# One kernel of attention and expert routing: the embedding loaded from another queue, fewer warming transposes, and a new hand-written order of steps

## The chip, the cores and the metric

The kernel runs on one core of a Trainium2 chip. A core has five engines with a queue of instructions each: TensorE (PE in the rows below; its weight loads are PEld), VectorE (DVE), ScalarE (ACT), GpSimd (POOL) and SyncE (SP), which here only issues transfers. The metric is the time of one execution in device microseconds; less is better. A difference is read against the runs of the kernel before, which lie between 472.85 and 473.6 us.

## The reference

Causal attention over 4 batches, 12 heads, 448 positions and 64 columns; its output, seen as 1792 tokens of 768 columns, goes through a layer of 8 experts, of which each token uses one.

```python
scores = scale * np.matmul(q, k.transpose(0, 1, 3, 2))
scores = np.where(mask, -1000000000.0, scores)
attn = np.exp(scores - np.max(scores, axis=-1, keepdims=True))
attn = attn / (np.sum(attn, axis=-1, keepdims=True) + 1e-09)
x = np.matmul(attn, v)                 # then laid out as 1792 x 768
...
xn = x / (np.linalg.norm(x, axis=-1, keepdims=True) + 1e-06)
en = expert_emb / (np.linalg.norm(expert_emb, axis=-1, keepdims=True) + 1e-06)
logits = xn @ en.T / tau
expert_idx = np.argmax(logits, axis=1)
...
for e in range(E):                     # w1: 768 x 1024, w2: 1024 x 768 for each expert
    mask = expert_idx == e
    h = np.maximum(x[mask] @ w1[e], 0.0)
    out[mask] = gate_w[mask, None] * (h @ w2[e])
```

## The kernel before

The work has two halves. In the first, 24 pairs of heads (numbered 0 to 23, six to a batch) go through attention, four chunks of 112 query rows each. In the second, the tokens, sorted by expert, go in tiles of 128 through the two weight matrices.

No scheduler sets the order. The string ORDER is a list of tokens such as `V3x.12/A` or `S1.4:0`: a step's name, a pair, after a slash the engine (A ScalarE, V VectorE, G GpSimd) where a step can be done by several, after a colon the PSUM banks. A loop at the end of `attn_moe` (L1001) calls the steps one after the other, and each engine runs its own instructions strictly in that order, waiting where a tile is not ready.

The steps of a pair `p`, chunk `i` and head `h`: `LDr`, `LDv` load queries with keys, and values (`LDa` is the first half of pair 0's `LDr`). `hi` and `lo` on GpSimd split the late columns into a rounded part and a rest (pairs 1 to 20). `S0` to `S3`, `S02` are the score products on TensorE. `M{i}{h}` on VectorE adds the mask and takes the row maximum out of PSUM. `E{i}{h}` on ScalarE is the exponential with its sum. `T0`, `T2`, `T3` transpose the result on TensorE into two tiles each, and `V0x`, `V0y` and so on copy these out of PSUM, on ScalarE or VectorE. `PV0` to `PV3` are the products with the values, `VO` copies their result, `RC` takes reciprocals of the sums, `X` turns the output to tokens and adds the products with the embedding, and `XE`, `LE` on VectorE scale both. Before that the embedding's norm is taken once: `EE` loads the embedding and tau on SP's queue, `es0` squares and sums on ScalarE, `es1` takes a first guess and two Newton steps of a square root on VectorE, `es2` to `esA` finish it.

At the end of a batch `R0` to `Rc` find each token's expert and its rank (`RK`, `CN` on TensorE). After the third batch `Z` picks the expert with the most tokens; its first matrix is loaded and split in six parts `k` (`LW` load, `W` rounded part on ScalarE, `Wl` rest: GpSimd for k below 5, VectorE for k = 5), and `Y`, `YP`, `YI`, `YG` gather a first tile of its tokens. `XTa` to `XLb` turn and split that tile. `F0` to `F5` are its first product on TensorE: `F0` to `F3` use part k of the weights, `F4` parts 4 and 5 for the first half of the columns, `F5` the same for the second. `RL` copies the halves out, `HT` transposes them, `HH` and `HL` split them. `A`, `B` split the second matrix (loads `LL`) on ScalarE and VectorE, `G1` to `G6` are parts of the second product. In between, on VectorE, `N0` to `Nc` work out the sorted place of every token, `TB` on TensorE turns that into a list, `IG` makes it integer, `GA` gathers the second tile, `xta` to `xlb` turn and split it. `Q` are sums of squares on ScalarE. From there on `body(t)` runs per tile, its order set by the code.

At the very start 16 transposes of the identity keep TensorE busy before the first scores (L999).

Of the kernel before, what the change touches and what calls it, by code (L numbers as in the profile page):

```python
# [45 lines left out]
V3y.1/V es4.0 M10.3 hi.3 V3x.1/A lo.3 S3.3:2 M11.3 es5.0 E31.2 S02.3:0 es6.0 M30.3 E01.2 hi.4 E20.2 T3.2:1 es7.0 M01.3
M20.3 es8.0 M31.3 lo.4 E11.2 PV0.1:6 PV1.1 V3x.2/A PV2.1 M21.3 PV3.1 RC.0/G E21.2 LDv.2 E00.2 es9.0:2 M00.3 E10.2
esA.0 T2.2:2 RC.1/G V3y.2/A VO.0/A T0.2:0 V2y.2/A V0y.2/A V2x.2/V S02.4:1 V0x.2/V LDr.7 X.0:2 M00.4 E01.3 M21.4 S3.4:0
PV0.2:7 E11.3 M01.4 E10.3 E20.3 E31.3 LE0.0 PV1.2 LDv.3 E30.3 LE1.0 XE1.0 M20.4 E00.3 E21.3 XE0.0 PV2.2 M30.4 M31.4
VO.1/V T3.3:1 RC.2/G lo.5 LDv.4 S1.4:0 V3y.3/V M11.4 M10.4 T0.3:2 PV3.2 V0y.3/V V3x.3/A S1.5:1 E20.4 V0x.3/A LDr.8  # L50
T2.3:0 S3.5:2 VO.2/A E21.4 V2y.3/A M10.5 E10.4 M11.5 E11.4 V2x.3/V M30.5 S02.5:1 M31.5 hi.6 lo.6 PV0.3:6 M21.5 M00.5
M01.5 X.1:2 E30.4 E00.4 M20.5 XE1.1 E11.5 E30.5 E01.4 T2.4:0 X.2:1 V2y.4/V LDv.5 E00.5 RC.3/G PV1.3 V2x.4/V XE1.2
LE1.2 E31.4 LE0.1 LDr.9 PV2.3 E01.5 LE0.2 XE0.1 E10.5 PV3.3 LE1.1 T0.4:0 XE0.2 V0x.4/A V0y.4/V T3.4:2 V3y.4/V V3x.4/A
S1.6:1 hi.8 M10.6 M11.6 S3.6:0 M31.6 S02.6:2 hi.7 E20.5 E21.5 M30.6 T0.5:1 PV0.4:7 M01.6 E31.5 M20.6 V0x.5/A M21.6
lo.7 T2.5:0 M00.6 V0y.5/A V2y.5/V T3.5:1 S02.7:2 RC.5/G VO.3/A V2x.5/A RC.4/G LDr.10 lo.8 V3x.5/A V3y.5/A S3.7:0 E01.6
M00.7 E30.6 M01.7 M21.7 E20.6 M20.7 M30.7 X.3:1 M31.7 LE1.3 XE1.3 S1.7:2 M11.7 XE0.3 PV1.4 PV2.4 PV3.4 E10.6 E11.6
LDv.6 E00.6 E21.6 M10.7 LE0.3 PV0.5:6 hi.9 T0.6:1 E31.6 V0y.6/A V0x.6/A LDr.11 VO.4/V T2.6:0 V2x.6/A X.4:2 V2y.6/V
E00.7 T3.6:1 E11.7 S02.8:0 PV1.5 E10.7 V3x.6/A E01.7 LDv.7 V3y.6/A PV2.5 lo.9 XE0.4 LE1.4 M00.8 M01.8 RC.6/G PV3.5
M20.8 XE1.4 LE0.4 E31.7 LDv.8 E00.8 S1.8:2 S3.8:1 M21.8 VO.5/V M11.8 X.5:0 M10.8 T0.7:2 XE1.5 PV0.6:7 E21.7 E21.8
LE0.5 hi.11 M31.8 E10.8 E20.7 PV1.6 E30.7 V0y.7/A LE1.5 V0x.7/V PV2.6 XE0.5 hi.10 E20.8 M30.8 PV3.6 T3.7:0 LDr.12  # L60
T2.7:2 VO.6/V V3x.7/A V3y.7/V V2y.7/A V2x.7/V S3.9:1 S02.9:0 M31.9 M30.9 E30.8 M01.9 E01.8 lo.10 S1.9:2 E31.8 q0.5
M11.9 E11.8 E01.9 PV0.7:7 hi.12 T3.8:1 M10.9 M21.9 X.6:2 R0.5:6 PV1.7 PV2.7 V3x.8/A V3y.8/A E30.9 PV3.7 XE0.6 RC.7/G
T0.8:1 M00.9 q3.5 q2.5 LE1.6 XE1.6 WX.5 q1.5 E31.9 LE0.6 M20.9 VO.7/A V0x.8/V LDr.13 T2.8:2 V0y.8/A V2x.8/A E11.9
E20.9 S3.10:0 V2y.8/V S02.10:1 E21.9 M30.10 M00.10 M01.10 LDv.10 E00.10 RC.8/G S1.10:2 PV0.8:7 M11.10 M31.10 M21.10
PV1.8 PV2.8 LDv.9 PV3.8 E00.9 lo.12 R1.5 E10.9 M20.10 T0.9:0 M10.10 R2.5 lo.11 R3.5 E21.10 S1.11:1 R4.5 X.7:2 M11.11
# [1116 lines left out]
```

## Time and profile before

| | us |
|---|---|
| time, median of 3 runs | 473.51 (472.85 to 473.6) |
| the profiled execution's own time | 474.17 |
| its span, first to last instruction | 472.0 |
| TensorE busy | 454.4 (96%) |
| VectorE busy | 349.3 (74%) |
| ScalarE busy | 295.9 (63%) |
| GpSimd busy | 158.0 (33%) |

The shares are means over stages that differ. Until about 160 us ScalarE, VectorE and TensorE are all close to full; after that TensorE alone is. A busy TensorE is not TensorE at its peak, since the modelled end of a matmul covers the time its result takes to come out.

### The profile page before, as it was taken

To read this page: it belongs to the slowest core of one execution; us is meant where nothing else is said; L and a number is where in the kernel's file an instruction comes from. 1 tells how busy PE (TensorE), PEld (TensorE's weight loads), DVE (VectorE), ACT (ScalarE), POOL (GpSimd) and SP (SyncE) were. 2 spreads that over 40 slices of the span, in tenths; PEclk is the share of its full clock that TensorE was granted. 3 is DMA by queue.
4 is the path that set the end of the run, shared out by engine and by line. 5 is a ranking of instruction groups with operands and counts; after the bars stand their busy time and mean duration, and the time that the engine had idled before them with its cause. 6 is when DMAs were issued, how large, how long until landed. Compare 5 with 4: busy or idle time off the path is not lost. (4 is left out here: it accounts for less than half of the span.)

```text
span 472.0 us, 12320 instructions
## 1 busy us (share of the span) xinstructions
PE 454.4 (96%) x3948; PEld 380.9 (81%) x3948; DVE 349.3 (74%) x1024; ACT 295.9 (63%) x731; POOL 158.0 (33%) x158
## 2 busy tenths in 40 slices
...
GB/s 181 206 102 92 169 179 120 138 216 118 150 134 276 269 124 97 69 33 164 174 378 294 296 52 267 76 392 223 301 330 227 110 69 56 284 180 283 286 250 38
DMA packets 27779, 87.35 MB, mean 185 GB/s; under 512 B 2710, under 2 KB 3670, under 8 KB 27680
## 3 DMA queue, kind: packets, MB, share of 16 engines
...
## 5 line engine op out<-in xcount | busy, mean ns | idle before, releaser
L425 ACT ACTIVATE aq<-aq,mx 112x224 f32<-112x224 f32 (+3 forms) x192 | 99.9, 529 | 2.4 <-DVE mx L420 2.3
...
L420 DVE CUSTOM_DVE_ANT_0 aq<-bank,ar 112x224 f32<-112x224 f32 (+3 forms) x192 | 76.0, 441 | 12.1 <-PE bank L415 10.6
L458 PE MATMUL bank<-ap 112*64 112x448 f32 (+3 forms) x384 | 53.2, 409 | 0.0
L721 DVE STREAM_TRANSPOSE turned<-fa 32x256 f32<-32x256 f32 x112 | 48.8, 436 | 1.8 <-DVE akr L733 0.3
L822 ACT COPY fa<-bank 128x512 f32<-128x512 f32 x28 | 15.2, 588 | 54.4 <-PE bank L763 40.3
L626 POOL DMA_INDIRECT fa<-xd,ig x21 | 23.7, 1129 | 62.8 <-PE bank L694 51.2
L443 PEld LDWEIGHTS bank<-idt,aq 64*112 64x112 f32 (+1 forms) x960 | 33.2, 131 | 13.9 <-ACT aq L425 4.4
L1030 DVE TENSOR_TENSOR wl<-fa,wh 128x1024 fp32r<-128x1024 f32 x36 | 41.5, 1218 | 3.1 <-PE bank L764 1.6
L447 ACT COPY ap<-bank 112x384 f32<-112x384 f32 (+2 forms) x91 | 39.5, 474 | 3.2 <-PE bank L443 1.6
L443 PE MATMUL bank<-idt,aq 48*112 48x48 f32 (+1 forms) x960 | 38.6, 219 | 2.3 <-ACT aq L425 1.0
L458 PEld LDWEIGHTS bank<-ap 112*64 112x64 f32 x384 | 23.8, 136 | 20.7 <-issue 12.6
L425 ACT ACTIVATION_READ_ACCUMULATOR aq<-aq,mx 112x1 f32 x192 | 37.8, 197 | 0.0
L1029 ACT CAST wh<-fa 128x1024 fp32r<-128x1024 f32 x36 | 34.9, 1048 | 3.5 <-PE bank L765 1.6
L763 PE MATMUL bank<-wh,akr 128*128 128x512 f32 x84 | 33.0, 393 | 0.0
L765 PE MATMUL bank<-wh,apr 128*128 128x512 f32 x84 | 32.9, 391 | 0.0
L765 PE MATMUL bank<-wh,akr 128*128 128x512 f32 x84 | 32.8, 391 | 0.0
L397 POOL TENSOR_TENSOR wl<-ak,wh 128x672 fp32r<-128x672 f32 x20 | 32.4, 1626 | 1.1
L764 PE MATMUL bank<-wl,akr 128*128 128x512 f32 x84 | 32.8, 391 | 0.0
L764 PE MATMUL bank<-wl,aor 128*128 128x512 f32 x84 | 32.8, 390 | 0.0
L763 PE MATMUL bank<-wh,aor 128*128 128x512 f32 x84 | 32.7, 389 | 0.0
L415 PE MATMUL bank<-ak 64*112 64x224 f32 (+3 forms) x224 | 31.3, 359 | 0.5 <-DVE ar L492 0.3
(320 smaller groups left out, 1172.8 us busy)
## 6 DMA issues: line engine op xcount, KB each, us to landing
...
```

Of the source, the lines that this page charges most:

```text
L397: step("lo", SPLIT)(lambda p: g.tensor_tensor(los[p % 3], late(p), his[p % 3], op=ALU.subtract))
L420: v.tensor_tensor_reduce(out=Ps[p % 2][i, h], in0=st.pop(("sp", p, i, h)), in1=mask[i], scale=-0.125, scalar=3e38, op0=ALU.add, op1=ALU.mi ...
L425: ac.activation(x, x, AF.Exp, bias=mxs[p % 3][:, h, i : i + 1], scale=-1.0, accum_out=sums[p % 3][:, h, i : i + 1])
L443: pe.transpose(t[:, h, k], Ps[p % 2][i, h][r, c * CP : c * CP + CP], idt[r, r], tile_position=(r.start, 0))
L447: copy()(PTs[p % 2][:, :, slice(*GROUPS[n]), ROWS[half]], st["pt", p, n][half])
L458: pe.matmul(st["o", p][64 * h : 64 * h + 64, CP * c : S], vts[p % 4][:, c, 64 * h : 64 * h + 64], PTs[p % 2][:, h, RUNS[c]], start=c == 0, ...
L721: v.transpose(xk[32 * j : 32 * j + 32, :, q : q + 32], blocks[q : q + 32, :, j])
L763: pe.matmul(acc[j], xh[:, k], wh[k][:, o], start=k == ends[0], stop=False)
L764: pe.matmul(acc[j], xh[:, k], wl[k][:, o], start=False, stop=False)
L765: pe.matmul(acc[j], xl[:, k], wh[k][:, o], start=False, stop=k == ends[1])
L1029: ac.copy(h[k], r[:, k])
L1030: v.tensor_tensor(l[k], r[:, k], h[k], op=ALU.subtract)
```

## The change

- The embedding and tau are loaded by ScalarE's queue, before ScalarE's table load, and no longer by SP's. The step `EE` is gone.
- `es1` does the guess and one Newton step; the second is a step of its own, `es1b`.
- 11 transposes at the start instead of 16.
- `Wl` takes its engine from ORDER. All six parts carry /G there, so part 5 moves from VectorE to GpSimd.
- `B` takes its engine from ORDER too, and no token names one, so all stay on VectorE.
- ORDER is new throughout. Copies `V` on ScalarE: 87 instead of 91, on VectorE 57 instead of 53; `VO` on ScalarE 16 instead of 17; `Rg` on ScalarE 4 instead of 2; `RC`'s first half on VectorE 5 times instead of 3; `Z2` goes to GpSimd and `Y0` to VectorE.

```diff
 ORDER = """
-LDa.0 LDr.0 S1.0:1 EE.0 es0.0 S3.0:0 S02.0:2 M11.0 M10.0 M31.0 LDr.1 M30.0 M20.0 M21.0 S1.1:1 M01.0 hi.1 E10.0 E31.0
...
-Rg.23/A N4.23 N5.23 R7.23 Ra.23
-Q0.23 A5.23 Q1.23 Rb.23 N6.23 N7.23 Wl4.17 F4.23 N8.23 RL0.23 Rc.23 N9.23 F5.23 Na.23 Nb.23 Nc.23 U0.23 B1.23 A0.23
-HTa.23:4 TB.23:2 IG.23 RL1.23 LL3.23 WX2.23 HHa.23 HLa.23 HTb.23:5 U1.23 GA.23 HHb.23 G1.23 G2.23 Q2.23 A6.23 U2.23
...
+es0.0 LDa.0 LDr.0 S1.0:2 LDr.1 es1.0 S02.0:1 M00.0 hi.1 lo.1 M10.0 M01.0 S3.0:0 M11.0 E00.0 E10.0 LDv.0 M20.0 M21.0
...
+N5.23 F2.23 N6.23 Rb.23 N7.23 N8.23 A5.23 N9.23 Rc.23 Na.23 Nb.23 Wl4.17/G F3.23 F4.23 RL0.23 A4.23 Nc.23 TB.23:5
+B3.23 IG.23 B2.23 U0.23 IU.23 LL3.23 HTa.23:4 Q3.23 GA.23 HHa.23 F5.23 U2.23 HLa.23 Q2.23 G1.23 U1.23 RL1.23 IS.23
...
         v.memset(es, 0.0)
-        ac.activation(es[:, 5:6], es[:, 5:6], AF.Exp)
...
-        @step("EE", FIRST)
-        def _(p):
-            sy.dma_start(er, emb)
-            sy.dma_start(es[:, 4:5], tau.broadcast_to([E, 1]))
-
+        ac.dma_start(er, emb)
+        ac.dma_start(es[:, 4:5], tau.broadcast_to([E, 1]))
+        ac.activation(es[:, 5:6], es[:, 5:6], AF.Exp)
...
-            for _ in range(2):
-                for f in newton(es[:, 2:3], es[:, 0:1], es[:, 2:3], es[:, 3:4]):
-                    f()
+            once()
+
+        def once():
+            for f in newton(es[:, 2:3], es[:, 0:1], es[:, 2:3], es[:, 3:4]):
+                f()
+
+        step("es1b", FIRST)(lambda p: once())
...
-            step(f"Wl{k}", STAR)(lambda p, k=k: (g if k < KD - 1 else v).tensor_tensor(l1[k], stage[k % 3], h1[k], op=ALU.subtract))
+            step(f"Wl{k}", STAR)(lambda p, k=k: vg().tensor_tensor(l1[k], stage[k % 3], h1[k], op=ALU.subtract))
...
-            step(f"B{k}", END)(lambda p, k=k: v.tensor_tensor(
+            step(f"B{k}", END)(lambda p, k=k: vg().tensor_tensor(
...
-        for _ in range(16):
+        for _ in range(11):
             pe.transpose(bx[:, :P], idt, idt)
```

Three places of the order follow, with the kernel before first each time. The lines of the changed kernel are one higher than those of the kernel before from L380 on, and one lower between L262 and L345.

VectorE at the start: `L420` (`L421`) are the masks `M`, `mx0` belongs to pair 0; `es` is the embedding's norm.

```order
L260 MEMSET es_82 8x6
L953 MEMSET ch_157 1x21
L420 ISA aq_77,mx0_139<-bank3_69,ar_79 112x224
L420 ISA mx0_139 112x1
L420 ISA aq_77,mx0_139<-bank2_68,ar_79 112x224
```

```order
L260 MEMSET es_82 8x6
L954 MEMSET ch_159 1x21
L349 TENSOR_SCALAR es_82<-es_82 8x1
L350 TENSOR_SCALAR es_82<-es_82 8x1
L320 TENSOR_SCALAR es_82<-es_82 8x1
L321 RECIPROCAL es_82<-es_82 8x1
L322 TENSOR_TENSOR es_82<-es_82 8x1
L323 TENSOR_TENSOR es_82<-es_82 8x1
L324 TENSOR_SCALAR es_82<-es_82 8x1
L421 ISA aq_77,mx0_138<-bank2_68,ar_79 112x112
L421 ISA mx0_138 112x1
```

The seven instructions of `es1` now stand ahead of the first mask; before, twelve stood behind the masks of pair 1.

VectorE where attention ends: `L487`, `L492` (`L488`, `L493`) are `XE` and `LE`, `L514` (`L515`) is `R0`, `L898` (`L899`) a step `B`, `L675` (`L676`) the steps `XL`.

```order
L675 TENSOR_TENSOR akr<-bank_69,akr 128x384
L675 TENSOR_TENSOR akr<-bank_71,akr 128x384
L492 TENSOR_TENSOR ar<-bank_67,R_138 112x4x8
L487 TENSOR_TENSOR fa<-bank_67,R_138 112x4x64
L898 TENSOR_TENSOR aqr<-fa,aqr 128x768
L487 TENSOR_TENSOR fa<-bank_70,R_138 112x4x64
L492 TENSOR_TENSOR ar<-bank_70,R_138 112x4x8
L487 TENSOR_TENSOR fa<-bank_71,R_138 112x4x64
L492 TENSOR_TENSOR ar<-bank_69,R_138 112x4x8
L492 TENSOR_TENSOR ar<-bank_71,R_138 112x4x8
L492 TENSOR_TENSOR ar<-bank_68,R_138 112x4x8
L514 TENSOR_REDUCE bank_72<-ar 112x32
```

```order
L676 TENSOR_TENSOR akr<-bank_71,akr 128x384
L493 TENSOR_TENSOR ar<-bank_66,R_137 112x4x8
L488 TENSOR_TENSOR fa<-bank_67,R_137 112x4x64
L493 TENSOR_TENSOR ar<-bank_67,R_137 112x4x8
L488 TENSOR_TENSOR fa<-bank_66,R_137 112x4x64
L493 TENSOR_TENSOR ar<-bank_69,R_137 112x4x8
L493 TENSOR_TENSOR ar<-bank_68,R_137 112x4x8
L488 TENSOR_TENSOR fa<-bank_71,R_137 112x4x64
L488 TENSOR_TENSOR fa<-bank_70,R_137 112x4x64
L493 TENSOR_TENSOR ar<-bank_70,R_137 112x4x8
L493 TENSOR_TENSOR ar<-bank_71,R_137 112x4x8
L515 TENSOR_REDUCE bank_73<-ar 112x32
```

One `B` (L898) is gone from between, and four instructions of pair 21 (bank_70, bank_71) now come last before `R0`; its `X` comes last on TensorE too, directly ahead of `F0`.

GpSimd where attention ends: `L604` (`L605`) are `Wl`, `L469` (`L470`) are halves of `RC`, `L626` (`L627`) the gathers.

```order
L604 TENSOR_TENSOR wl_75<-fa,wh_74 128x1024
L469 TENSOR_SCALAR sum_143<-sum_143 112x8
L626 DMA fa<-xd,ig_121 128x768
L469 TENSOR_SCALAR sum_142<-sum_142 112x8
L604 TENSOR_TENSOR wl_75<-fa,wh_74 128x1024 x2
L469 TENSOR_SCALAR sum_144<-sum_144 112x8
L604 TENSOR_TENSOR wl_75<-fa,wh_74 128x1024 x2
L626 DMA fa<-xd,ig 128x768 x3
```

```order
L605 TENSOR_TENSOR wl_75<-fa,wh_74 128x1024
L627 DMA fa<-xd,ig_120 128x768
L605 TENSOR_TENSOR wl_75<-fa,wh_74 128x1024
L470 TENSOR_SCALAR sum_142<-sum_142 112x8
L605 TENSOR_TENSOR wl_75<-fa,wh_74 128x1024 x4
L627 DMA fa<-xd,ig 128x768 x3
```

Six `Wl` stand where five stood, the last four in a row: parts 1, 5, 3, 4.

## Rows read from the trace of the kernel before

**Rows 1.** Busy us and instructions of each engine by stretch, granted clock, DMA
```profile
core 0: us, PE busy (x) PEld busy (x) DVE busy (x) ACT busy (x) POOL busy (x), PEclk, DMA share, GB/s
0.00:4.00 4.00, 2.56 (x12) 2.56 (x13) 0.11 (x2) 1.49 (x2) 3.12 (x19) 1.00 0.38 114
9.50:161.60 152.10, 149.97 (x2214) 109.20 (x2214) 139.38 (x627) 146.64 (x496) 97.67 (x96) 1.00 0.49 161
161.60:182.30 20.70, 18.42 (x114) 15.63 (x113) 19.66 (x62) 12.59 (x23) 8.60 (x5) 1.00 0.54 166
182.30:460.00 277.70, 275.62 (x1522) 248.05 (x1521) 185.79 (x321) 130.82 (x200) 43.85 (x36) 1.00 0.56 205
```

**Rows 2.** Timeline, 0 to 15 us: start, us, instruction, idle before and its releaser
```profile
0.81 1.28 ACT L261 ACT_TABLE_LOAD   x1 [0.81 <-PEq L1169]
...
1.44 3.68 PE L1000 MATMUL bank<-idt 128*128 128x128 f32 x16 [1.44 <-POOL idt masks.py:199]
...
2.20 0.53 SPq L345 DMA_DIRECT2D fa<-in_emb_dram  x1
...
5.05 3.37 PE L415 MATMUL bank<-ak 64*112 64x224 f32 x20
5.30 0.84 ACT L348 ACTIVATE fa<-fa 8x768 f32<-8x768 f32 x1 [2.99 <-DMA fa<-in_emb_dram]
...
6.31 0.39 DVE L420 CUSTOM_DVE_ANT_0 aq<-bank,ar 112x224 f32<-112x224 f32 x1 [5.33 <-PE bank L415]
...
7.06 0.48 ACT L425 ACTIVATE aq<-aq,mx 112x224 f32<-112x224 f32 x1 [0.83 <-DVE mx L420]
...
13.59 0.13 DVE L352 TENSOR_SCALAR es<-es 8x1 int32<-8x1 int32 x1
...
14.84 0.14 DVE L321 TENSOR_SCALAR es<-es 8x1 f32<-8x1 f32 x1
```

**Rows 3.** Copies by line, whole span or 0 to 162 us: count, busy us, mean ns
```profile
L447 ACT COPY ap<-bank 112x384 f32<-112x384 f32 (+2 forms) x91 | 39.5, 474 | 3.2 <-PE bank L443 1.6
...
L447 DVE COPY ap<-bank 112x384 f32<-112x384 f32 (+2 forms) x53 | 26.9, 529 | 2.9 <-PE bank L443 2.7
...
L447 ACT COPY ap<-bank 112x288 f32<-112x288 f32 x30 | 12.0, 400 | 0.8 <-PE bank L443 0.5 <-DVE ap L447 0.2
...
L464 ACT COPY ao<-bank 128x448 f32<-128x448 f32 x17 | 9.1, 534 | 1.0 <-PE bank L458 1.0
...
L517 ACT COPY Lg<-bank 112x32 f32<-112x32 f32 x1 | 0.2, 170 | 0.0
```

**Rows 4.** Timeline, 160 to 168 us: ScalarE's VO.23, VectorE's Wl5, GpSimd's Wl3 and Wl4
```profile
160.00 0.53 ACT L464 COPY ao<-bank 128x448 f32<-128x448 f32 x1 [1.02 <-PE bank L458]
...
164.51 2.89 DVE L604 TENSOR_TENSOR wl<-fa,wh 128x1024 fp32r<-128x1024 f32 x1
...
161.56 4.77 POOL L604 TENSOR_TENSOR wl<-fa,wh 128x1024 fp32r<-128x1024 f32 x2 [3.03 <-ACT wh L603]
```

**Rows 5.** Line 1030, the same subtraction later: count, ns minimum, median, maximum
```profile
L1030 DVE TENSOR_TENSOR wl<-fa,wh x36: 1206/1217/1260, 233.6 to 421.8; 128x1024 fp32r<-128x1024 f32 x36
```

**Rows 6.** Timeline of VectorE, 162 to 168 us: R0, R5, N0
```profile
162.15 0.97 DVE L514 TENSOR_REDUCE bank<-ar 112x32 f32<-112x384 f32 x1
...
164.07 0.19 DVE L521 TENSOR_TENSOR O<-bank,rmx 112x32 f16<-112x32 f32 x1
...
167.67 0.15 DVE L918 TENSOR_SCALAR ni<-bank 112x8 int32<-112x8 f32 x1
```

**Rows 7.** Timeline of TensorE, 161 to 183 us: F0, TB, G1's third, xta, next tile
```profile
161.61 0.50 PE L763 MATMUL bank<-wh,akr 128*128 128x512 f32 x1
...
172.20 0.56 PE L942 MATMUL bank<-M,turned 112*128 112x42 f16 x16 [0.43 <-DVE M L936]
...
173.99 0.44 PE L765 MATMUL bank<-akr,aqr 128*128 128x384 f32 x1 [0.24 <-DVE aqr L685]
...
179.06 0.87 PE L672 MATMUL bank<-idt,fa 128*128 128x128 f32 x6 [0.98 <-DMA fa<-xd,ig]
...
182.32 0.39 PE L763 MATMUL bank<-wh,aor 128*128 128x512 f32 x1
```

More of the change, by code (lines that the diff above doesn't have):

```diff
@@ L46 @@
[L46 to L65, printed above, removed]
@@ L106 @@
-V3y.22/V E30.23 X.20:1 T2.23:0 V2x.22/V V2y.22/V V2y.23/V V2x.23/V XE1.20 PV3.21 PV0.22:7 RC.22/G PV1.22 PV2.22 PV3.22
-LL1.23 E11.23 T3.23:2 W1.17 LE1.20 YG.17 LDv.23 XE0.20 RC.21/G E00.23 VO.21/A LW3.17 LE0.20 T0.23:1 X.21:0 A2.23
-VO.22/V Wl2.17 V0x.23/A Wl1.17 V3x.23/A V3y.23/V V0y.23/V A3.23 XTb.23:3 XE0.21 XHb.23 B2.23 XTa.23:5 LE0.21 RC.23/G
-PV0.23:7 XLb.23 XHa.23 XLa.23 PV1.23 PV2.23 LE1.21 PV3.23 XE1.21 VO.23/A X.22:2 LW5.17 B3.23 XE0.22 X.23:1 LW4.17
-LE0.22 F0.23 XE1.22 LE1.23 LE1.22 LL0.23 LE0.23 W3.17 R0.23:6 R1.23 W4.17 R2.23 Wl3.17 W5.17 R3.23 R4.23 R5.23 XE0.23
@@ L111 @@
-Wl5.17 F1.23 RK.23 WX1.22 F2.23 A4.23 XE1.23 N0.23 R6.23 A1.23 N1.23 N2.23 N3.23 F3.23 Rg.23/A N4.23 N5.23 R7.23 Ra.23
-Q0.23 A5.23 Q1.23 Rb.23 N6.23 N7.23 Wl4.17 F4.23 N8.23 RL0.23 Rc.23 N9.23 F5.23 Na.23 Nb.23 Nc.23 U0.23 B1.23 A0.23
-HTa.23:4 TB.23:2 IG.23 RL1.23 LL3.23 WX2.23 HHa.23 HLa.23 HTb.23:5 U1.23 GA.23 HHb.23 G1.23 G2.23 Q2.23 A6.23 U2.23
-B4.23 HLb.23 A7.23 U3.23 G3.23 IU.23 U4.23 U5.23 G4.23 H0.23 xta.23:3 Q3.23 xtb.23:4 xha.23 H1.23:5 B5.23 G5.23 B6.23
-B7.23 xla.23 B0.23 xhb.23 H2.23 G6.23 xlb.23 IS.23
+es0.0 LDa.0 LDr.0 S1.0:2 LDr.1 es1.0 S02.0:1 M00.0 hi.1 lo.1 M10.0 M01.0 S3.0:0 M11.0 E00.0 E10.0 LDv.0 M20.0 M21.0
@@ new lines @@
+RC.22/G Wl1.17/G XE0.19 PV2.22 LE1.19 V2y.23/A XE0.20 E01.23 LW3.17 LE1.20 LE0.20 V2x.23/V XE1.20 T3.23:0 E10.23
+T0.23:1 V3y.23/V XTa.23:5 LW4.17 V0y.23/V XTb.23:4 PV3.22 A1.23 V3x.23/A VO.22/V V0x.23/A XHb.23 PV0.23:7 W5.17 PV1.23
+B1.23 RC.23/V XHa.23 PV2.23 PV3.23 XLb.23 VO.23/A XLa.23 X.22:0 X.23:1 LE0.22 X.21:2 XE1.22 LE1.22 XE0.22 LE1.23
+LE0.23 XE1.21 XE0.21 LE0.21 W3.17 LE1.21 R0.23:7 R1.23 R2.23 R3.23 F0.23 R4.23 W4.17 LL1.23 Wl5.17/G R5.23 A3.23 F1.23
+Rg.23/A XE1.23 RK.23 XE0.23 N0.23 N1.23 LL2.23 Wl3.17/G N2.23 A2.23 R6.23 N3.23 A0.23 WX1.22 N4.23 R7.23 WX2.23 Ra.23
```

111 lines of the change are left out of this document (67 added, 44 removed).

## Prediction

> **What bounds the kernel now.** I read the table by stretch first. From 182.3 to 460 us TensorE is busy for 275.62 of 277.70 us [rows 1]; nothing of the change stands there, so whatever is won or lost before 182.3 should reach the end whole. Before that there are two stretches. From 161.6 to 182.3 VectorE is busy for 19.66 of 20.70 us and TensorE for 18.42 [rows 1]: a hand-over in which VectorE works out places of tokens for which TensorE waits. From 9.5 to 161.6, attention, TensorE is busy for 149.97 of 152.10 us, ScalarE for 146.64 and VectorE for 139.38 [rows 1]. TensorE's share is the highest, but its modelled ends overlap, and its weight loads fill only 109.20. I take ScalarE, idle for 5.46 us, as the engine that sets the pace, with TensorE as a rival. So three places have to be priced: the start, attention, and the hand-over. I count from the first matmul of F0, at 161.61, called T0 [rows 7].
>
> **The start.** The 16 transposes run from 1.44 to 5.12 and the first scores start at 5.05 [rows 2], so they wait for the queue, not for data: the DMA engines had moved 4.00 us x 114 GB/s = 456 KB by 4.0 us [rows 1], and the two loads of pair 0 are 2 x 224 KB. One transpose takes 3.68 / 16 = 0.23 us, five 1.15, so TensorE can begin at about 4.0. That does not reach VectorE whole, since seven instructions of es1 now stand ahead of its first mask. The embedding was issued at 2.20 and used at 5.30, 3.10 later [rows 2]. ScalarE's queue, whose table load starts at 0.81 [rows 2], can issue it at about 0.85, so it lands at 3.95. The table load, 1.28 us, comes behind two issues (0.53 for the row shown, less for tau) and ends by 3.2, so it is hidden; without that cover it would cost what passes 3.95. es0 takes 0.93 (0.84 and its sum's read), and seven instructions 14.84 - 13.59 = 1.25 [rows 2]: the first mask starts at 3.95 + 0.93 + 1.25 = 6.1 to 6.2, against 6.31 before. The first exponential then comes some 0.35 later, about 6.55 against 7.06, as the first chunk is now the 112-column one: 0.5 us won on ScalarE. VectorE wins 0.1 and the 1.25 that it no longer spends at 13.59. Bounds: if the embedding lands as late as before, at 5.30, the first mask starts at 7.5 and ScalarE loses 0.8; if it lands sooner, TensorE's first scores bind (4.0 plus the 6.31 - 5.05 = 1.26 that they took), first mask at 5.3, 1.3 won. TensorE may be slower at its first products after fewer transposes; es1 leaves it about 0.9 us of room.
>
> **Attention.** The steps are the same, so what can be counted is who does them. ScalarE gives up four copies net (91 to 87). The columns say which: one 384 more, four 288 and one 512 fewer, so near four of the small form, 4 x 0.400 = 1.60, and at most 4 x 0.474 = 1.90 [rows 3]. One VO less is 0.534, two Lg copies more are 0.34 [rows 3]. Together 1.8 to 2.1; these means contain some 0.1 us each that overlaps the next instruction, so I take 1.5. VectorE takes over five copies at 0.529 = 2.65 [rows 3], two halves of RC and Y0 for about 0.5 (priced by the 0.15 to 0.19 of the small rows [rows 6]), loses two Lg copies and Z2, about 0.5, and es1's 1.25: +1.4 on an engine that was idle for 152.10 - 139.38 = 12.7 us. The rest of ORDER is a permutation whose waits no row shows. ScalarE's idle time of 5.46 bounds what it can win; I allow 2.5 us either way and take nothing. In attention's last microseconds W5 moves ahead of VO.23 on ScalarE, into a wait of 1.02 us that is there now [rows 4], so I cost it at nothing; if that wait is gone it costs about 1.05. GpSimd stood idle for 3.03 us ahead of Wl3 [rows 4], and Wl5 (4.77 / 2 = 2.39) fits in. B1 now stands ahead of XLb and XLa, which F0 needs; in the old order they were done some 1.8 us before T0, and B1 takes the place of B2, so nothing is lost. T0 comes 0.5 + 1.5 = 2.0 us earlier, with bounds of +1.5 and -5.
>
> **The hand-over,** counted from T0. Before: R0 at +0.54, R5 done at +2.65, N0 at +6.06, TB at +10.59, G1's third matmul at +12.38, xta at +17.45 after 0.98 of waiting for the gather, next tile at +20.71 [rows 6, 7]. Between R5 and N0 lies Wl5 on VectorE, 2.89 us [rows 4], where the same instruction later takes 1.217 [rows 5]. It leaves VectorE. Two things run against that. X.21 is now the last product before F0, so four more VectorE instructions come after T0: R0 starts at about +1.1, R5 ends at +3.2, and RK, behind F1 (F0 and F1 are done at +2.9), makes TensorE wait 0.3. Then XE1.23 and XE0.23 (0.75), so N0 at +3.95 instead of +6.06; the chain from N0 to TB takes 172.20 - 167.67 = 4.5, and TB can start at +8.5.
>
> Wl5 took 164.51 + 2.89 = 167.40, its usual 1.217 after 166.2, and GpSimd's Wl4 ended at 161.56 + 4.77 = 166.33 [rows 4, 5]: VectorE's subtraction of two SBUF tiles stood until GpSimd's was over. *The Trainium skill, "SBUF — State Buffer", section "Who interferes with whom", says the same: a VectorE instruction with two SBUF inputs contends with a GpSimd instruction that reads SBUF, and whichever issues first holds the shared ports for its whole length.* *By that rule the move speaks against itself: GpSimd, given one more Wl, would hold up the N chain, which has ten such instructions.* From the rows: Wl5 can start when W5 ends, about T0 - 2, so Wl3 runs from +0.4 and Wl4 ends at 0.4 + 2 x 2.39 = +5.2. N2, due at +4.3, waits 0.9, and TB comes at +9.4.
>
> TensorE reaches F4's end at about +7.65 (F2 at +3.5, three steps of 1.38), stands for 0.8 to 1.7 us, runs TB (0.56), HTa (0.45), F5 (1.38), and then G1, whose third matmul needs HLa. On VectorE B3, B2 and small ones (0.95 x 2 + 0.8) lie ahead of HLa, so that matmul starts at +11.6 to +12.4, where it was at +12.38. What follows is HTb (0.45, earlier before), the rest of G1 and G2 to G4 (3.9), H1, xta, xtb and G5, G6 (3.4): 7.7 us instead of 8.33, since the gather, issued some 2 us sooner, has landed. The next tile starts at +19.3 to +20.1 instead of +20.71: 0.6 to 1.4 us won. I take 1.0.
>
> **Sum.** 2.0 + 1.0 = 3.0 us less. The profiled execution took 474.17 us, a span of 472.0 and 2.17 around it; it would become 471.2. It stands 0.66 above the median of 473.51, so the median becomes 470.5. The bounds give 468.3 (all the start, 1.9 of copies, 0.5 fewer waits, 1.4 of hand-over) to 472.2 (1.3 won in all).
>
> **Rivals.**
> 1. *TensorE sets attention's pace.* For it: 149.97 of 152.10 busy, and no matmul of attention is removed. Against: weight loads fill 109.20, and VectorE and ScalarE have little idle time [rows 1]. Then only the 0.1 of the start counts, and 0.7 of hand-over: 472.7, no change.
> 2. *VectorE becomes the bound, and it is slower.* VectorE's 12.7 idle us are mostly forced (it waits for fresh scores), and five copies of 0.529 at moments when a mask is due push the mask, then the exponential, then the transposes. The price is the +1.4 of above less 0.1, plus one or two subtractions held up by GpSimd for up to 2.39 - 1.22 = 1.2 each, less 0.6 of hand-over: about +1.5, so 475.0. It decides as soon as more than half of the copies that moved land in front of a mask for which ScalarE stands idle. Against: ScalarE's idle time is small in every part of attention now.
> 3. *The shared ports eat the hand-over.* W5 comes a microsecond later than I put it (1.05 instead of in the gap), Wl4 ends at +6.3, N2 waits 2 us, TB comes at +10.5: nothing is won after T0. *It is the rule of the skill's page in full.* With attention's 2.0: 471.5. The rows show it once (2.89 for 1.217), so it is real; whether the times meet is open.
> 4. *The start does not do what it says:* the embedding lands late, ScalarE loses 0.8 instead of winning 0.5: 471.8. It goes into the first range.
>
> **How the numbers follow.** Forecast 0.56, rival 1 0.17, rival 2 0.15, rival 3 0.12. A measurement of this kernel can tell about 0.2%, 0.95 us, from no change, so faster is below 472.56. Forecast and rival 3 are faster: 0.68. Rival 1 is the same: 0.17. Rival 2 is slower: 0.15. The range takes in the forecast from 468.5, rivals 1 and 3 whole, and rival 2 up to 474.3, about a third of it: 468.5 to 474.3 leaves out about 0.15.
>
> **What would show each step.** Start: the first mask at 6.1 to 6.2 behind es1, the first exponential before 6.7, no transposes after 4.1. Attention: F0 at about 159.6, ScalarE busy about 145 us from 9.5 us to there. If rival 1, F0 at 161.3 with ScalarE's idle time up by 1.5; if rival 2, F0 later than 162 and ScalarE waiting for masks. Hand-over: TB 8.5 to 9.4 us after F0, no VectorE row of 2.89, an N instruction of 0.17 stretched to a microsecond, and the next tile 19.3 to 20.1 after F0. What makes it wrong most easily is the permutation of 24 pairs, which I priced at zero because no row prices it.

## The result, and the profile of the changed kernel

The change made the kernel slower. Four executions of the changed kernel took 475.15 to 478.91 us, median 477.86, beside 473.23 before: a ratio of 1.0075 (95% interval 1.0051 to 1.0100). The ratio is estimated from the executions of both kernels and is not the quotient of the two medians, which is 1.0098. Run again (e1 below) the kernel took 478.5 against 473.74, 1.0098 (1.0082 to 1.0114). The forecast was 470.5 with a range of 468.5 to 474.3. Every ratio below is against the kernel before on the same chip, and the intervals are 95%. One execution each of e2 and e4 lay more than 1.5% above the shortest of its kernel; it is in the median and not in the ratio.

The profile is that of the shortest of the four executions: 475.15 us, a span of 473.3. Its first view is the table by stretch, with the columns of [rows 1].

```profile
9.50:165.20 155.70, 151.16 (x2208) 109.56 (x2208) 143.55 (x619) 145.41 (x489) 100.73 (x95) 0.98 0.48 155
165.20:184.40 19.20, 18.22 (x114) 15.57 (x113) 18.02 (x63) 12.05 (x24) 7.24 (x5) 1.00 0.58 186
184.40:462.00 277.60, 275.74 (x1521) 248.15 (x1521) 186.08 (x319) 130.57 (x200) 43.58 (x36) 1.00 0.57 205
```

Attention lasts until 165.2 us, not 161.6, although ScalarE is busy for 1.2 us less in it than in [rows 1]; the granted clock (PEclk) is 0.98 where it was 1.00. The hand-over shrank from 20.7 to 19.2 us. The stretch behind it is as before, and from there to the end of the span it is 288.9 us instead of 289.7. So the loss is in attention, where F0 was to come 2.0 us earlier and comes 3.6 later.

The timeline of the changed kernel's start, to hold against [rows 2]:

```profile
1.44 2.61 PE L1001 MATMUL bank<-idt 128*128 128x128 f32 x11 [1.44 <-POOL idt masks.py:199]
...
3.16 0.83 ACT L345 ACTIVATE fa<-fa 8x768 f32<-8x768 f32 x1
...
3.98 3.12 PE L416 MATMUL bank<-ak 64*112 64x224 f32 x16
...
6.50 0.27 DVE L421 CUSTOM_DVE_ANT_0 aq<-bank,ar 112x112 f32<-112x112 f32 x1 [1.17 <-PE bank L416]
...
6.82 0.39 ACT L426 ACTIVATE aq<-aq,mx 112x112 f32<-112x112 f32 x1 [2.74 <-DVE mx L421]
```

The embedding is there by 3.16 and the scores start at 3.98. The first mask still waits 1.17 us, for TensorE: it now takes the first chunk, whose product stands behind others in the queue. The first exponential comes at 6.82, 0.24 earlier than before.

Next, the place of the loss. These are rows of three engines' timelines near 135 us, where `Z`, which picks the first expert, meets GpSimd's `qa0`, `qa1` and `qb` (halving sums of the second batch's squares):

```profile
133.44 5.49 POOL L563 TENSOR_TENSOR fa<-fa 112x768 f32<-112x768 f32 x3
...
134.27 1.01 DVE L550 TENSOR_SCALAR jt<-pi 112x4 int32<-112x4 int32 x1
135.20 1.87 DVE L583 TENSOR_SCALAR star<-star,zmx 112x8 f32<-112x8 f32 x1
...
137.29 0.14 DVE L588 CAST mt<-zmx 1x1 int32<-1x1 f32 x1
137.36 1.59 DVE L589 TENSOR_SCALAR nstar<-star 112x8 f32<-112x8 f32 x1
...
138.96 0.44 DVE L448 COPY ap<-bank 112x288 f32<-112x288 f32 x1
...
139.46 1.83 PE L416 MATMUL bank<-ak 64*112 64x448 f32 x2 [2.54 <-DVE ap L448]
141.22 5.44 PE L459 MATMUL bank<-ap 112*64 112x448 f32 x28
```

In the kernel before, `Z4` and the end of `Z5` are over when the halving sums start:

```profile
136.75 0.23 DVE L582 TENSOR_SCALAR star<-star,zmx 112x8 f32<-112x8 f32 x1
...
137.28 0.19 DVE L588 TENSOR_SCALAR nstar<-star 112x8 f32<-112x8 f32 x1
...
137.39 5.49 POOL L562 TENSOR_TENSOR fa<-fa 112x768 f32<-112x768 f32 x4
```

In the changed kernel GpSimd works from 133.44 to 138.93, and three VectorE instructions of a few columns (`Ra`, `Z4`, the end of `Z5`) take 1.01, 1.87 and 1.59 us. Undisturbed, rows of theirs are 0.16, 0.23 and 0.15 to 0.19. Each is over within 0.05 us of the end of one of GpSimd's three halving sums, which end at 135.26, 137.04 and 138.92. That is 3.9 us of VectorE, and behind them in its queue stands the copy of 138.96, for which TensorE waits 2.54 us. Two more VectorE rows of this profile are stretched, both of the embedding's norm: 1.50 us for 0.15 at 11.09 (`es1b`) and 1.60 us for 0.60 at 27.17 (`es8`); the kernel before has one such row ahead of F0, 1.47 us at 19.52. The table by stretch shows what follows the wait:

```profile
139.00:145.00 6.00, 5.54 (x16) 2.16 (x18) 5.70 (x29) 2.62 (x10) 0.86 (x3) 0.50 0.51 175
146.00:147.00 1.00, 1.00 (x26) 0.81 (x24) 0.00 (x0) 0.00 (x0) 0.59 (x1) 1.00 0.00 0
```

After TensorE's idle time the granted clock is 0.50, the lower level of 1.2 GHz, for six us. The 28 products at 141.22 take 5.44 us; with the clock at 1.00 the same 28 take 3.24 (in the runs below).

Last the hand-over on TensorE, for [rows 7]: F0, TB, next tile.

```profile
165.23 0.50 PE L764 MATMUL bank<-wh,akr 128*128 128x512 f32 x1
...
173.77 0.56 PE L943 MATMUL bank<-M,turned 112*128 112x42 f16 x16 [0.41 <-DVE M L937]
...
184.40 0.39 PE L764 MATMUL bank<-wh,aor 128*128 128x512 f32 x1
```

Counted from F0, TB comes at +8.54 (before +10.59) and the next tile at +19.17 (before +20.71).

### The profile page after: what moved, and what is told of

The parts are those of the page before. It is cut to its first block, busy times and chain, and to the rows that moved or that the text cites. A ratio compares the mean times of both kernels' runs of the same rounds, so it can differ in the third digit from the quotient of the medians.

```text
span 473.3 us, 12300 instructions
## 1 busy us (share of the span) xinstructions
PE 455.2 (96%) x3943; PEld 380.6 (80%) x3943; DVE 353.2 (75%) x1028; ACT 294.4 (62%) x728; POOL 158.8 (34%) x157
## 5 line engine op out<-in xcount | busy, mean ns | idle before, releaser
L426 ACT ACTIVATE aq<-aq,mx 112x112 f32<-112x112 f32 (+3 forms) x192 | 100.1, 531 | 6.2 <-DVE mx L421 5.6
L421 DVE CUSTOM_DVE_ANT_0 aq<-bank,ar 112x224 f32<-112x224 f32 (+3 forms) x192 | 76.2, 442 | 4.6 <-PE bank L416 3.5
L459 PE MATMUL bank<-ap 112*64 112x112 f32 (+3 forms) x384 | 54.7, 421 | 0.8 <-ACT aq L426 0.8
L459 PEld LDWEIGHTS bank<-ap 112*64 112x64 f32 x384 | 25.1, 140 | 25.2 <-issue 16.8
L627 POOL DMA_INDIRECT fa<-xd,ig x21 | 22.5, 1073 | 64.0 <-PE bank L695 52.3
L448 DVE COPY ap<-bank 112x384 f32<-112x384 f32 (+2 forms) x57 | 28.9, 527 | 6.1 <-PE bank L444 6.1
```

Of the source, the lines that this page charges most:

```text
L421: v.tensor_tensor_reduce(out=Ps[p % 2][i, h], in0=st.pop(("sp", p, i, h)), in1=mask[i], scale=-0.125, scalar=3e38, op0=ALU.add, op1=ALU.mi ...
L426: ac.activation(x, x, AF.Exp, bias=mxs[p % 3][:, h, i : i + 1], scale=-1.0, accum_out=sums[p % 3][:, h, i : i + 1])
L448: copy()(PTs[p % 2][:, :, slice(*GROUPS[n]), ROWS[half]], st["pt", p, n][half])
L459: pe.matmul(st["o", p][64 * h : 64 * h + 64, CP * c : S], vts[p % 4][:, c, 64 * h : 64 * h + 64], PTs[p % 2][:, h, RUNS[c]], start=c == 0, ...
```

## The experiments

Two theories were held against each other. By theory L ("lock") VectorE's instructions on SBUF tiles stand still while GpSimd runs a long instruction on SBUF tiles, and the new order makes the two meet. By the rivals, the new order or the shortened start leaves TensorE without work in any case.

| run | what it is | median us | ratio |
|---|---|---|---|
| e1_again | the changed kernel | 478.5 | 1.0098 (1.0082 to 1.0114) |
| e2_nolock | Z behind the halving steps | 475.36 | 1.0034 (1.0015 to 1.0054) |
| e3_warm | 20 transposes into TensorE's gap | 476.08 | 1.0056 (1.0036 to 1.0075) |
| e4_nolock_es | e2 and `es1b` earlier | 475.89 | 1.0025 (0.9997 to 1.0054) |
| e5_noq | changed, no halving steps of pair 17 | 471.74 | 0.9953 (0.9934 to 0.9972) |
| e6_noq_norc | e5, no addition in RC | 468.24 | 0.9886 (0.9862 to 0.9909) |
| e7_before_noq_norc | before, with e6's two omissions | 478.88 | 1.0108 (1.0084 to 1.0132) |
| e8_apart | changed, VectorE and GpSimd kept apart | 469.39 | 0.9908 (0.9884 to 0.9932) |
| e9_apart_es | e8, `es8` and Y0 on GpSimd | 470.24 | 0.9920 (0.9897 to 0.9942) |
| e10_before_y0 | before, Y0 on VectorE | 477.9 | 1.0100 (1.0065 to 1.0135) |
| e11_before_start | before, with the new start | 473.93 | 1.0001 (0.9984 to 1.0018) |
| e12_apart_wl5 | e8, Wl5 on VectorE | 472.71 | 0.9964 (0.9945 to 0.9983) |

### e1: the changed kernel again

> The changed kernel as it is, once more. Theory: near 138 us VectorE stands behind GpSimd, TensorE stands idle behind VectorE, its granted clock falls to 0.50 for some microseconds, and how long it stays there differs from run to run. So 475 to 479 us again, with the stall at the same instructions in the profile (136.9 to 139.5 us) and a granted clock below 1 behind it. Rival (the new order is slower throughout, and the stall is only its largest wait): the same time, but a profile of another execution need not show the stall there.

It was 478.5. The profiled execution (478.56 us) has the three stretched rows near 135 us and the fall of the clock behind them, and a second meeting, just ahead of F0. GpSimd's three `Wl` run from 162.79 to 169.98; VectorE's and TensorE's timelines read:

```profile
163.03 2.33 DVE L470 TENSOR_SCALAR sum<-sum 112x8 f32<-112x8 f32 x1
...
166.29 1.47 PE L483 MATMUL bank<-ar,ao 64*112 64x72 f32 x16 [1.01 <-DVE akr L676]
```

This is `RC.23`, the addition of 1e-9 to eight sums, which the change moved from GpSimd to VectorE. In the profile shown first the same instruction started at 162.26, took 0.17 us, and GpSimd's first `Wl` started at 162.42. So 0.2 us of relative position goes with 2.2 us of VectorE, one way in which executions of the changed kernel can differ. Executions of the kernel before differ too: beside e1, 23 of them lie between 472.87 and 476.78 us.

### e2, e3, e4: moving Z, filling the gap

```diff
 e2: ORDER (on VectorE: Ra.11, Z4, Z5, R7, Y0, Y1 behind GpSimd's halving steps in time)
-... Z3.17 Ra.11 Z4.17 E10.21 ... Z5.17 R7.17 ... Y0.17 M11.22 PV1.19 M31.22 Y1.17 M30.22 PV2.19 M01.22 ...
+... Z3.17 E10.21 ... M11.22 PV1.19 M31.22 M30.22 PV2.19 M01.22 Ra.11 Z4.17 Z5.17 R7.17 Y0.17 Y1.17 ...
 e3: ahead of step S3.22, into a free PSUM bank
+            if token == "S3.22":
+                for _ in range(20):
+                    pe.transpose(bank[7][:, :P], idt, idt)
 e4: ORDER as e2, and
-es0.0 ... es1.0 S02.0:1 ... T3.0:1 es1b.0 M31.1 ...
+es0.0 ... es1.0 es1b.0 S02.0:1 ... T3.0:1 M31.1 ...
```

> The changed kernel with six small VectorE steps (Ra of pair 11; Z4, Z5, R7, Y0, Y1 of pair 17) moved behind the masks of pair 22, so that VectorE has no subtraction, sum or scaling between two SBUF tiles to do while GpSimd runs its three long sums of squares (qa, qb). Theory (ports, then the clock): the rows of 1.01, 1.87 and 1.59 us become 0.16 to 0.23, TensorE does not stand from 136.9 to 139.5, the clock stays at 1.00, F0 comes 5 to 7 us earlier than at 165.2, and the time is 468 to 471 us with runs within 1 us of one another. Rival (the new order is slower in itself): at most the 2.5 us of TensorE's idle time come back, F0 at 162.5 or later, 473 or more.

> The changed kernel with 20 transposes of the identity on TensorE ahead of S3 of pair 22, in the bank that R6 has just released, so that TensorE is not idle while it waits for VectorE; nothing else. Theory: VectorE's long rows stay, TensorE still cannot go on before 139.5, but the clock stays at 1.00, and the time is less by what the half clock costs: it stood at 0.50 for 6.7 us in the profile, up to 3.3 us; 472 us, runs closer together. Rival (the clock only follows the idle time and costs nothing of its own): 475 to 479 as before, plus nothing.

> As the run without the meeting at 134 us, and the second Newton step (es1b) moved right behind the first, into the 1.17 us for which VectorE waits for its first scores. In the changed kernel its row at 11.09 took 1.50 us for 0.15 while GpSimd ran a lo step. Theory: 0.9 + 1.35 us come off VectorE near 11 us; as ScalarE follows VectorE there, up to 1 us earlier at F0 than without it, 467.5 to 470.5. Rival (attention is paced by ScalarE or TensorE): no difference to the run without it beyond 0.3 us.

All three missed; each won only a part. In e2 `Z4` is back at 0.22 us, but the meeting has only moved, and a new wait came with it. VectorE's and ScalarE's timelines:

```profile
136.21 1.62 DVE L470 TENSOR_SCALAR sum<-sum 112x8 f32<-112x8 f32 x1
...
146.69 1.05 ACT L604 CAST wh<-fa 128x1024 fp32r<-128x1024 f32 x1 [3.31 <-DMA fa<-in_w_dram]
```

`RC.20` now stands in the halving steps, 1.62 us. And since Z5 gives the expert's number later, the first weight part is loaded later, and ScalarE waits 3.31 us for it. `RC.23` stands 2.33 us as well. In this profile the clock stays at 1.00 up to F0, and F0 comes at 165.00 all the same.

e3 leaves the meeting and fills TensorE's gap:

```profile
138.48 2.40 PE L1010 MATMUL bank<-idt 128*128 128x128 f32 x20 [1.02 <-DVE pos L537]
...
141.75 3.24 PE L459 MATMUL bank<-ap 112*64 112x448 f32 x28
```

The clock stays at 1.00 and the 28 products take 3.24 us. The time is (1.0098 - 1.0056) x 474 = 2.0 us shorter, where 472 had been expected. So the clock is a second price of the stall, and the smaller one. In e4 the second Newton step no longer meets GpSimd (in e1 two of its instructions took 1.49 and 0.65 us near 11 us); the intervals of e4 and e2 overlap, so that meeting has no price that these runs show.

### e5, e6, e7: what meets taken away, in both kernels

```diff
 e5, e7: ORDER, pair 17
-qa0.17 ... qa1.17 ... qb.17 ... qc.17 ... qd.17
 e6, e7: RC
-            vg().tensor_scalar(x, x, 1e-9, None, ALU.add)
             v.reciprocal(Rs[p // PB % 2][:, p % PB], x)
```

> The changed kernel without GpSimd's five halving steps of the second batch's sums of squares (qa0, qa1, qb, qc, qd of pair 17); it leaves out that part of the sum. Everything else stands where the change put it. Theory L (VectorE's tensor_scalar instructions stand still while GpSimd works on two SBUF tiles): jt, Z4 and Z5 take 0.16 to 0.23 us again, TensorE's idle time between 136 and 147 us goes, F0 starts near 161 to 162 instead of 165 to 168, and the time is 472 to 474.5; pair 23's sum (VectorE, line 470) may still meet GpSimd's low parts for 2.3 us in some executions. Rival C (the new order, or the shorter warming, starves TensorE whatever GpSimd does): the gap stays in another form, 475 to 478.

> As the run before it, and also without the addition of 1e-9 to the sums of the exponentials (RC's tensor_scalar of all pairs; the sums are 1 or more, so f32 does not show the addition). Theory L: no VectorE tensor_scalar is left that can meet GpSimd in attention except those of the embedding's scale near 11 and 27 us; F0 at 159.5 to 161.5, time 469.5 to 472, with a narrower spread. Rival C: no more than 0.5 below the run without the halving steps.

> The kernel before with the same two things left out (the five halving steps of pair 17, RC's addition in all pairs). Theory L: the kernel before lost no more than 1.3 us of VectorE to this anywhere ahead of 186 us, and that off the path, so it stays at 472.5 to 474. Rival (less work on GpSimd and VectorE helps any order alike): 469 to 471, as much won as in the changed kernel.

e5 is (1.0098 - 0.9953) x 474 = 6.9 us shorter than the changed kernel. What it leaves out is 7.2 us of GpSimd, an engine that is idle for two thirds of the span. Its timeline has `Z4` and `Z5` whole again, one meeting that is left, and F0:

```profile
156.27 2.33 DVE L469 TENSOR_SCALAR sum<-sum 112x8 f32<-112x8 f32 x1
...
160.92 0.50 PE L763 MATMUL bank<-wh,akr 128*128 128x512 f32 x1
```

e6 takes that last one away too and wins (0.9953 - 0.9886) x 473.4 = 3.2 us more. Not all of this need be the instruction of 156.27: e6 leaves out the addition on both engines, GpSimd's 19 of 24 included, and in its profile `es8` has its 0.60 us again (1.78 in e5). F0 comes at 157.03, 4.6 us earlier than before [rows 7], and no row of VectorE between 12 and 157 us is stretched by more than 0.3 us. Both were better than theory L had put them (472 to 474.5, and 469.5 to 472).

e7 missed, and is the most telling. The same two omissions make the kernel before 5 us slower. GpSimd's timeline in the kernel before, and behind it GpSimd's, VectorE's and TensorE's in e7:

```profile
85.01 0.23 POOL L469 TENSOR_SCALAR sum<-sum 112x8 f32<-112x8 f32 x1 [2.06 <-ACT aq L425]
...
86.02 3.22 POOL L397 TENSOR_TENSOR wl<-ak,wh 128x672 fp32r<-128x672 f32 x2
```

In e7:

```profile
83.46 3.20 POOL L396 TENSOR_TENSOR wl<-ak,wh 128x672 fp32r<-128x672 f32 x2
...
84.00 2.68 DVE L547 TENSOR_SCALAR jt<-pi 112x4 int32<-112x4 int32 x1
...
87.11 1.07 PE L442 MATMUL bank<-idt,aq 48*112 48x48 f32 x27 [1.98 <-DVE mx L419]
```

Before, `RC` on GpSimd waits 2.06 us for ScalarE's sums, and that holds the two `lo` back until 86.02; VectorE's `Ra` ran at 83.3 in 0.16 us. Without RC the two `lo` start at 83.46, `Ra` stands for 2.68 us, and TensorE waits 1.98. A wait that looked like waste kept two engines apart. In that execution, the shortest of e7 (476.88), F0 comes at 164.6, 3.0 us later than before. VectorE's other stretched rows lie between 18 and 25 us (2.8 us above their usual length, of which the kernel before has 1.3 too); they were not tried one by one.

### e8, e9: the whole work, kept apart

```diff
 e8
-            vg().tensor_scalar(x, x, 1e-9, None, ALU.add)
-        step("Z4", STAR)(lambda p: v.tensor_scalar(star, star, zmx, None, ALU.is_equal))
+        step("Z4", STAR)(lambda p: vg().tensor_scalar(star, star, zmx, None, ALU.is_equal))
-            v.tensor_scalar(nstar, star, -1.0, 1.0, ALU.mult, ALU.add)
+            g.tensor_scalar(nstar, star, -1.0, 1.0, ALU.mult, ALU.add)
 ORDER: Z4.17/G; es1b.0 behind es1.0; Rb.17 Ra.17 Y2.17 Rc.17 Y3.17/G behind VO.20/A
 e9, besides
-        step("es8", FIRST)(lambda p: v.tensor_scalar(ej, er, es[:, 3:4], None, ALU.mult))
+        step("es8", FIRST)(lambda p: g.tensor_scalar(ej, er, es[:, 3:4], None, ALU.mult))
 ORDER: Y0.17/G
```

> The changed kernel, whole work, with GpSimd and VectorE kept apart: RC's addition left out (no change in f32), Z4 and the inverted mark of Z5 on GpSimd ahead of its sums of squares, Ra, Rb, Y2, Rc and Y3 of pair 17 behind the copy of pair 20, and the second half of the embedding's scale right behind the first. Theory L: none of jt, Z4, Z5, RC or the scale is stretched before 165 us, F0 at 160 to 162.5, time 470 to 473, below the kernel before. Rival C: 475 or more.

> As e8_apart, and also es8 (the embedding's scaling, 8x768, which VectorE took 2.05 us for near 27 us in that trace) and Y0 (1.36 us near 141) on GpSimd. Theory L: no VectorE row in attention is stretched any more, TensorE does not wait 1.20 us near 29 us, so the granted clock stays at 1.00 from 30 to 40 us; time 467.5 to 469.5 with a spread under 2 us. Rival (GpSimd's longer queue now makes scores or transposes of the embedding wait): 470 to 472.

e8 does the whole work (the sums are 1 or more, so an addition of 1e-9 changes nothing in f32) and is faster than both kernels: 469.39 us, 0.9908. It is 1.9% below the changed kernel, and below the 470 to 473 expected. Z4 and the mark on GpSimd hold GpSimd's own halving steps back until Z has what it needs.

The profiled execution of e8 is its longest (473.65; the other five 468.44 to 471.12), and shows two meetings that are left: Y0 near 141 us (1.36 us), and the scaling of the embedding, which had been expected to go. Rows of VectorE and TensorE for the second:

```profile
27.10 2.05 DVE L367 TENSOR_SCALAR fa<-fa,es 8x768 f32<-8x768 f32 x1
...
29.21 0.53 PE L374 MATMUL bank<-idt,fa 8*128 8x8 f32 x6 [1.20 <-DVE fa L367]
```

The stretch behind it, columns as in [rows 1]:

```profile
32.00:36.00 4.00, 4.00 (x42) 3.50 (x38) 2.29 (x9) 3.31 (x11) 1.03 (x1) 0.50 0.02 4
```

The scaling of the embedding (0.60 us undisturbed) meets a `lo`, TensorE waits 1.20 us, and the clock is at 0.50 from 31 to 37 us. e9 wanted to take that away and won nothing that shows (the intervals overlap): on GpSimd the scaling took longer than it had stood on VectorE, and TensorE still waited 0.72. The clock did stay at 1.00 from 30 to 40 us, as expected, but it was 0.50 from 12 to 14.

```profile
27.20 2.21 POOL L367 TENSOR_SCALAR fa<-fa,es 8x768 f32<-8x768 f32 x1 [10.38 <-DVE es L365]
```

With Y0 gone from VectorE, `Rc` came into the halving steps instead and stood 2.27 us for 0.68. The time is in the rival's range; of its reason the trace shows those 0.72 us.

### e10: one token in the kernel before

```diff
-RC.19/G V3x.20/V Y0.17/G LDv.21 R6.17
+RC.19/G V3x.20/V Y0.17/V LDv.21 R6.17
```

> The kernel before with one token changed: Y0 of pair 17 on VectorE, not on GpSimd. It is the only thing that holds GpSimd's halving steps behind Z4 there, so they start near 136.2 instead of 137.4 and meet Z4, Z5 and Y0. Theory L (this meeting is enough to make the loss): Z4, Z5's last instruction and Y0 take 1 to 2 us each, VectorE loses 3 to 4 us, F0 comes 2 to 4 us later, 475.5 to 478. Rival (the loss needs the new order around it): 473 to 474, no different from before.

477.9 us, 1.0100 (1.0065 to 1.0135): a loss as large as that of the change, by one letter. In the kernel before GpSimd's Y0 waits for Z4 and so holds the halving steps behind it:

```profile
137.07 0.37 POOL L608 TENSOR_TENSOR ob__148<-O,star 112x96 f32<-112x96 f16 x1 [0.93 <-DVE star L582]
```

In e10, GpSimd, then VectorE, then F0 on TensorE:

```profile
136.21 5.45 POOL L561 TENSOR_TENSOR fa<-fa 112x768 f32<-112x768 f32 x4
...
136.34 1.71 DVE L579 TENSOR_TENSOR star<-star,r 112x8 f32<-112x8 f32 x1
...
138.28 1.67 DVE L581 TENSOR_SCALAR star<-star,zmx 112x8 f32<-112x8 f32 x1
...
140.24 0.77 DVE L587 TENSOR_SCALAR nstar<-star 112x8 f32<-112x8 f32 x1
...
166.49 0.50 PE L762 MATMUL bank<-wh,akr 128*128 128x512 f32 x1
```

The halving steps start 1.2 us earlier, meet Z, and F0 is 4.9 us later than in [rows 7], more than the 2 to 4 expected. Z2 stood where Y0 had been expected to. So this meeting is enough, without the new order around it.

### e11, e12: the start and the hand-over alone

```diff
 e11: the kernel before; step EE and its token gone
+        ac.dma_start(er, emb)
+        ac.dma_start(es[:, 4:5], tau.broadcast_to([E, 1]))
+        ac.activation(es[:, 5:6], es[:, 5:6], AF.Exp)
-        for _ in range(16):
+        for _ in range(11):
 e12: e8 with, in ORDER
-Wl5.17/G
+Wl5.17/V
```

> The kernel before with the changed kernel's start alone: embedding and tau issued from ScalarE's queue, 11 warming transposes; es1 and the order stay. The prediction's term: scores from 4.0 us, first exponential 0.5 us or so earlier, 472.5 to 473.5. Rival 1 (fewer transposes let the clock fall or the first load sets the first score anyway): first exponential within 0.3 us of before, 473.3 to 475. Rival 2 (an earlier start shifts engines against one another and makes new meetings of VectorE with GpSimd further on): 474 or more, with stretched tensor_scalar rows in the trace.

> As e8_apart, but Wl5 on VectorE as in the kernel before. The prediction's hand-over term: Wl5 stands 2.4 to 2.9 us on VectorE behind GpSimd's Wl4 between R5 and N0, TB comes 9.5 to 10.6 us after F0 instead of 8.5, the next tile 1.0 to 1.8 us later after F0; time 470.2 to 471.2 against e8_apart's 469.4. Rival (the hand-over is set by TensorE's own work): the next tile within 0.3 us of 19.2 after F0, 469 to 469.8.

e11: 1.0001 (0.9984 to 1.0018). The start does what it says, and at the end it is worth nothing; 472.5 to 473.5 had been expected and 473.93 came. GpSimd's first `hi` in the kernel before, which waits for the load of pair 1:

```profile
7.08 0.75 POOL L396 CAST wh<-ak 128x672 fp32r<-128x672 f32 x1 [2.68 <-DMA ak<-in_qk_dram]
```

In e11, VectorE's first mask and ScalarE's first exponential, GpSimd's first `hi`, TensorE's next scores, and F0:

```profile
5.15 0.39 DVE L417 CUSTOM_DVE_ANT_0 aq<-bank,ar 112x224 f32<-112x224 f32 x1 [4.17 <-PE bank L412]
...
5.90 0.48 ACT L422 ACTIVATE aq<-aq,mx 112x224 f32<-112x224 f32 x1 [1.82 <-DVE mx L417]
...
7.95 0.74 POOL L393 CAST wh<-ak 128x672 fp32r<-128x672 f32 x1 [3.56 <-DMA ak<-in_qk_dram]
...
7.95 0.64 PE L412 MATMUL bank<-ak 64*112 64x224 f32 x4 [1.46 <-DMA ak<-in_qk_dram]
...
10.44 0.41 PE L412 MATMUL bank<-wl,wh 64*112 64x336 f32 x2 [1.02 <-POOL wl L394]
...
161.81 0.50 PE L760 MATMUL bank<-wh,akr 128*128 128x512 f32 x1
```

The first exponential is 1.16 us earlier than in [rows 2]. TensorE then waits 1.46 us for a load of queries and keys and 1.02 us for GpSimd's `lo`, for neither of which it waited before, and F0 stands where it stood. The load is there later, not at the same time: the first `hi` starts at 7.95 instead of 7.08. In the three profiles with the embedding on SP's queue (the kernel before, e7, e10) it starts at 6.85 to 7.12, in the eleven with it on ScalarE's at 7.17 to 7.98. Why the load lands later was not tried.

e12 is 0.56% above e8, 2.7 us, more than the 1.0 to 1.8 expected; the two intervals do not overlap. VectorE and TensorE:

```profile
162.53 1.99 DVE L604 TENSOR_TENSOR wl<-fa,wh 128x1024 fp32r<-128x1024 f32 x1
...
164.89 0.19 PE L529 MATMUL bank<-Os,ones 112*112 112x40 f16 x1 [2.30 <-ACT Lg L517]
...
170.95 0.57 PE L942 MATMUL bank<-M,turned 112*128 112x42 f16 x16
```

F0 was at 159.56, so TB came at +11.39, against +8.53 in e8. The place is not quite that of the kernel before: in the new order Wl5 stands ahead of R5 and so delays RK too, for which TensorE waits 2.30 us; then the granted clock is 0.67 from 165 to 170 us. So Wl5 on GpSimd is worth at least what was forecast here, and in this order more.

## Why the prediction was wrong, point by point

**The start: -0.5 forecast, 0 measured (e11).** Transposes and scores came as worked out (4.05, 3.98); the embedding, put at 3.95, was there by 3.16. Two steps failed. The first mask was put behind `es1` alone, at 6.1 to 6.2, and waited for the product of the first chunk until 6.50. And a gain at the first exponential was carried to the end, while in e11 the next load, which lands later than before, takes it back. e11 keeps `es1` at its old place, so the new place has no price of its own.

**ScalarE's copies: -1.5.** ScalarE's busy time up to F0 came out as said (about 145; 145.41). F0 was forecast at 159.6 and came at 165.23, and at 167.68 in e1. With the meetings taken away it comes at 157.03 (e6), 160.20 (e9) and, in the whole-work e8's longest execution, 163.44. That the new order can be a gain is shown: without the meetings it is 5.4 us faster than the kernel before (e6, with a little work left out), 4.4 with the whole work (e8). How much of this is the copies' is not: no run moved the copies alone, and the kernel before was not rearranged in the same way.

**The waits of the permutation: 0 ± 2.5 forecast; this is the step that failed.** Leaving out the halving steps, which meet Z, is worth 6.9 us (e1 to e5), leaving out RC's additions 3.2 (e5 to e6). I took the permutation as something no row prices, but two of its moves could be read from it. Y0 goes from GpSimd to VectorE, and with it the wait that held the halving steps back: in the kernel before this alone costs 4.7 us (e10, 0.0100 x 473.84; 4.1 by the medians). And RC.3, RC.4, RC.19 and RC.23 go to VectorE, where RC.20 was already (RC.9 and RC.13 leave it), RC.23 beside GpSimd's longest instructions: it stood 2.33 us in the profiles of e1 to e5 and not in the one shown first; I priced the two halves of RC by rows of 0.15 to 0.19 us. I had the mechanism at hand, from the 2.89 for 1.217 of Wl5 [rows 4, 5], and used it for subtractions only. *The Trainium skill, "SBUF — State Buffer", section "Who interferes with whom", names `tensor_scalar` among the VectorE operations that can take the ports it shares with GpSimd, next to operations with two SBUF inputs; I drew on the second half of that rule and not on the first.* *The trace agrees with both: 1.87 us for 0.23 (Z4, tensor_scalar), 1.71 for 0.17 (Z2 in e10, two SBUF inputs).*

**The hand-over: -1.0 forecast, -0.6 to -1.5 measured.** TB at +8.5 to +9.4 (measured +8.54), no row of 2.89, no stretched N instruction, next tile at +19.3 to +20.1 (+19.17). The mechanism was right and a little undersized, since nothing had to wait for GpSimd's Wl4. In e1, e3 and e4, where the clock is at 0.50 as F0 starts, the next tile comes at +19.73 to +20.10.

**The rivals.** Rival 2 (VectorE becomes the bound) named the right engine and direction, at 475.0, and the wrong cause: not the copies, but the instructions that I had counted at 0.15. It had one or two held subtractions in its price, and its own terms run from +0.7 with none to +3.1 with two held in full, so that +1.5 was a choice below the middle. Rival 1 does not hold: TensorE ends attention earlier as soon as VectorE is free. Rival 3 placed the shared ports in the hand-over, where no row of the changed kernel is held; they cost ahead of it, near 135 us and, in e1, just before F0.

**Where the gain went.** Forecast -3.0 (and 468.3 at best, where the terms named give 5.1 and so 468.4); the halving steps and RC cost +10.1 together, and the order without them is worth 5.4 and not 3.0: -5.4 + 10.1 = +4.7, which is e1's loss (the two sizes are differences of e1, e5 and e6, so the sum has to close). A part of the 10.1 is the clock's, 2.0 us by e3.

**Open.** In the profiles of e1, e3, e9 and e12 the granted clock falls between 10 and 16 us too; in those of the first profile, e2, e6 and e8 it does not. e11 has 11 transposes and the old order and its profile keeps 1.00 there, so the shorter warming need not bring it about; more transposes in the new order were not tried. What is left of the spread in e8 and e9 may come from there.
